# Moving the wait for the output from SyncE to GpSimd at the end of a decode kernel, without GpSimd's closing drain

## The chip, the cores and the metric

The kernel runs on one core of a Trainium2 chip. The time is device microseconds of one execution. "The span" is the time from the first to the last instruction of the program that the profile shows; the measured time is longer than the span.

Names: PE is TensorE, DVE VectorE, ACT ScalarE, POOL GpSimd, SP SyncE; SPq or POOLq is an engine's sequencer, which carries out branches, drains and semaphore instructions. L578 is line 578 of the kernel.

## The reference

One decode step of a transformer layer for four sequences, in bfloat16: layer norm, attention with 32 heads over a cache of 4096 positions, output projection, residual; then layer norm, a SwiGLU feed-forward block, residual.

```python
def reference(A_x, A_k_cache, A_v_cache, A_wq, A_wo, B_x, B_w_gate, B_w_up, B_w_down):
    x = A_x                                                     # (4, 1, 640)
    h = x + _A_ref(_layernorm(x), A_k_cache, A_v_cache, A_wq, A_wo)   # caches (4, 32, 4096, 192)
    h2 = h + _B_ref(_layernorm(h), B_w_gate, B_w_up, B_w_down)  # 640 -> 1536 -> 640
    return h2
```

## The kernel before

SP streams the K and V caches in loads of 6 MB, DVE and PE work on them in loops. None of that is touched. What matters is the end: the last cast, four small output DMAs (two issued by SP, two by ACT), and a recording layer that writes each engine's program into one block. SP is the engine that waits for the output.

```python
    def emit(self, block, final):
        # ... dependencies become semaphore values (cut)
        def run(eng):
            def body(e):
                # ... this engine's instructions with their waits (cut)
                if eng == "sp":
                    for d in final:
                        e.wait_ge(d.sem, d.value)
            return body
        block.vector(run("dve")); block.gpsimd(run("pool")); ...   # (cut)

    # ... end of build_kernel:
    a = op("dve", lambda e: e.tensor_copy(out=outsb[:, 0:DQ], in_=psH[:, 0:DQ]), [a])
    fin = [dma("sp" if n < 2 else "act", lambda e, n=n: e.dma_start(
        out[:, 0, n * DQ:(n + 1) * DQ], outsb[32 * n:32 * n + B, 0:DQ]), S_out, [a]) for n in range(4)]

    with nc.Block() as block:
        pr.emit(block, [fin[-1]])
```

The end of a block is a barrier, which the built program spells out. Each engine branches to the block's end (the profiles show a branch only where it carries a wait). DVE, ACT, PE and SP drain, and the drain's semaphore update is the engine's arrival. GpSimd drains, collects the four arrivals (one semaphore instruction) and releases the others (a second one). The others pass (one each). "Arrival", "collect", "release" and "pass" are used for these below. SP's wait for the output is attached to SP's branch.

## Time and profile before

| | before |
|---|---|
| measured time, median of the first three runs | 989.99 us (989.90 to 990.32) |
| measured time of the profiled run, its span | 989.84 us, 988.26 us |
| HBM traffic | 424.29 MB read, 429 GB/s |
| last cast ends, output landed, last pass | 985.89, 987.66, 988.26 us |

Lines of the profile page before: the span; busy time by engine; the main DMA queue with packets, MB and its share of sixteen engines' span; the chain of work that ended last, by engine.

```profile
span 988.3 us, 9469 instructions
...
PE 579.3 (59%) x4409; PEld 129.0 (13%) x2941; DVE 553.3 (56%) x454; ACT 117.1 (12%) x376; POOL 3.7 (0%) x18
...
q1 hardware_dynamic: 10528, 424.29, 99.5%
...
DMA 67%; PE 18%; DVE 12%; issue 1%; SPq 1%; DVEq 0%
```

DMA is busy from end to end, no engine is; the kernel is bound by its 424 MB. GpSimd does 3.7 us of work, all at the start.

The instructions of the closing line before. The columns are engine and operation, count, duration in ns (lowest, median, highest), and the start of the first and the last in us.

```profile
L578 POOLq EVENT_SEMAPHORE  x2: 17/17/17, 987.9 to 987.9; - x2
L578 POOLq DRAIN  x1: 611/611/611, 4.9 to 4.9; - x1
...
L578 ACTq DRAIN  x1: 239/239/239, 986.8 to 986.8; - x1
L578 SPq COMPARE_BRANCH  x1: 33/33/33, 987.7 to 987.7; - x1
L578 SPq DRAIN  x1: 7/7/7, 987.8 to 987.8; - x1
L578 ACTq EVENT_SEMAPHORE  x1: 17/17/17, 988.0 to 988.0; - x1
L578 PEldq EVENT_SEMAPHORE  x1: 51/51/51, 988.0 to 988.0; - x1
L578 DVEq EVENT_SEMAPHORE  x1: 21/21/21, 988.0 to 988.0; - x1
L578 SPq EVENT_SEMAPHORE  x1: 17/17/17, 988.2 to 988.2; - x1
```

Two lines of SP's waits before (who waited for whom, us in total, times, longest):

```profile
SPq L578 <- DMA out_dram<-gu: 1.1, 1, 1.1
SPq L578 <- SPq L578: 0.4, 1, 0.4
```

GpSimd's drain ran at 4.9 us. SP's branch comes when the output has landed, at 987.7. Everyone passes at 988.0 but SP, which passes at 988.2 and so ends the span; the second wait line is that lateness, seen from SP's drain.

The view rounds starts to 0.1 us. Where finer times stand below, they are the records of the trace, in us after the landing of the last output increment (987.661 before): branch of SP 0.017, its drain 0.158, collect 0.190, release 0.269, passes of ACT, PE, DVE 0.315 to 0.322, pass of SP 0.586, end of span 0.603. SP's branch is recorded only once its wait is over. This agrees with the Trainium skill, "Perfetto Trace Analysis", section "Sequencer-only Instruction (DRAIN, etc)": the profiler reports such an instruction from when its semaphores are satisfied.

### The profile page before, as it was taken

To read this page: it belongs to the slowest core of one execution; us is meant where nothing else is said; L and a number is where in the kernel's file an instruction comes from. 1 tells how busy PE (TensorE), PEld (TensorE's weight loads), DVE (VectorE), ACT (ScalarE), POOL (GpSimd) and SP (SyncE) were. 2 spreads that over 40 slices of the span, in tenths; PEclk is the share of its full clock that TensorE was granted. 3 is DMA by queue.
4 is the path that set the end of the run, shared out by engine and by line. 5 is a ranking of instruction groups with operands and counts; after the bars stand their busy time and mean duration, and the time that the engine had idled before them with its cause. 6 is when DMAs were issued, how large, how long until landed. Compare 5 with 4: busy or idle time off the path is not lost.

```text
span 988.3 us, 9469 instructions
## 1 busy us (share of the span) xinstructions
PE 579.3 (59%) x4409; PEld 129.0 (13%) x2941; DVE 553.3 (56%) x454; ACT 117.1 (12%) x376; POOL 3.7 (0%) x18
## 2 busy tenths in 40 slices
PE   1677555666555576556566655656665555765554
PEld 0011011110101111001111110111101011110023
DVE  2486555566645556655556665555666455566621
ACT  0311111110111110011111011111101111100120
POOL 1000000000000000000000000000000000000000
PEclk9898777887777888777788777788877778887775
DMA  9999999999999999999999999999999999999997
GB/s 401 428 440 426 434 436 426 440 434 430 436 426 440 434 432 436 426 438 434 432 436 426 438 434 432 436 426 438 434 432 436 426 438 434 432 436 426 438 433 327
DMA packets 10583, 424.39 MB, mean 429 GB/s; under 512 B 1232, under 2 KB 1232, under 8 KB 1744
## 3 DMA queue, kind: packets, MB, share of 16 engines
q1 hardware_dynamic: 10528, 424.29, 99.5%
q8 instruction: 5, 0.08, 0.0%
q10 hardware_dynamic: 48, 0.01, 0.0%
q14 instruction: 2, 0.02, 0.0%
HBM read 424.29 MB, written 0.01 MB: 429 GB/s over the span
## 4 chain that ended last, share of the span: by engine, by line
DMA 67%; PE 18%; DVE 12%; issue 1%; SPq 1%; DVEq 0%
DMA k<-in_A_k_cache_dram 63%; DVE prod L412 12%; PE pb L161 11%; PE pb L462 4%; DMA wd_sb<-in_B_w_down_dram 4%; PE pb L420 2%; SPq L365 0%; DVE sc L425 0%; PE pb L468 0%; DVEq L412 0%; SPq L391 0%; SPq L385 0%; PE pb L571 0%; SPq L330 0%; PE pb L434 0%
## 5 line engine op out<-in xcount | busy, mean ns | idle before, releaser
L412 DVE TENSOR_TENSOR prod<-k,qball 128x6144 f16<-128x6144 bf16 x128 | 426.3, 3351 | 220.9 <-DMA k<-in_A_k_cache_dram 220.9
L161 PE MATMUL pb<-prod,identH 128*128 128x512 f16 x1408 | 384.3, 429 | 0.0
L420 PE MATMUL pb<-prod,identH 128*128 128x512 f16 x128 | 58.1, 454 | 339.9 <-DVE prod L412 339.9
L425 DVE TENSOR_REDUCE sc<-pb 128x32 f32<-128x512 f32 x128 | 88.0, 688 | 107.2 <-PE pb L161 107.2
L477 ACT ACTIVATE otmp<-pb,minv 128x192 f32<-128x192 f32 x32 | 13.4, 420 | 650.8 <-PE pb L462 650.8
L420 PEld LDWEIGHTS pb<-prod,identH 128*128 128x128 f16 x128 | 13.2, 103 | 586.1 <-DVE prod L412 481.2
L462 PE MATMUL pb<-v,pbuf 128*8 128x384 bf16 x1984 | 86.0, 326 | 0.0
L453 ACT ACTIVATE pbuf<-sc,negM 32x128 bf16<-32x128 f32 x128 | 73.4, 574 | 4.9
L462 PEld LDWEIGHTS pb<-v,pbuf 128*8 128x8 bf16 x1984 | 45.4, 87 | 28.8
L481 DVE SCALAR_TENSOR_TENSOR orow<-pb,minv,otmp 128x192 f32<-128x192 f32 x32 | 13.4, 418 | 55.1 <-ACT otmp L477 55.1
L497 PEld LDWEIGHTS pb<-orow,here 128*128 128x128 f32 x256 | 33.5, 192 | 73.7 <-issue 71.1
L497 PE MATMUL pb<-orow,here 128*128 128x48 f32 x256 | 31.7, 267 | 1.1 <-DVE orow L481 1.1
L453 ACT ACTIVATION_READ_ACCUMULATOR pbuf<-sc,negM 32x1 f32 x128 | 31.7, 248 | 0.0
L447 ACT ACTIVATE negM<-pb 128x4 f32<-128x4 f32 x32 | 5.5, 173 | 161.0 <-PE pb L443 161.0
L468 PEld LDWEIGHTS pb<-lsb,headm 128*128 128x128 f32 x64 | 12.3, 194 | 74.8 <-issue 71.2
L443 PE MATMUL pb<-negMc,ones_row 1*128 1x4 f32 x64 | 12.2, 258 | 11.9 <-DVE negMc L438 11.9
L434 PE MATMUL pb<-identF,msb 128*1 128x128 f32 x64 | 12.1, 270 | 9.8 <-DVE msb L430 9.8
L438 DVE TENSOR_REDUCE negMc<-pb 1x4 f32<-1x128 f32 x32 | 8.9, 279 | 15.1 <-PE pb L434 15.1
L443 PEld LDWEIGHTS pb<-negMc,ones_row 1*128 1x128 f32 x64 | 9.4, 183 | 21.3 <-DVE negMc L438 21.3
L468 PE MATMUL pb<-lsb,headm 128*128 128x1 f32 x64 | 9.2, 213 | 2.7 <-ACT pbuf L453 2.7
L490 ACT ACTIVATE here<-place 128x131 f32 (+1 forms) x32 | 10.0, 312 | 0.9
L430 DVE TENSOR_REDUCE msb<-sc 128x1 f32<-128x128 f32 x32 | 9.1, 286 | 1.1
(68 smaller groups left out, 84.8 us busy)
## 6 DMA issues: line engine op xcount, KB each, us to landing
k<-in_A_k_cache_dram SPq DMA_DIRECT2D x32, 6144.0 KB, 39.5
v<-in_A_v_cache_dram SPq DMA_DIRECT2D x31, 6144.0 KB, 25.5
wq_sb<-in_A_wq_dram SPq DMA_DIRECT2D x1, 7680.0 KB, 21.5
k<-in_A_v_cache_dram SPq DMA_DIRECT2D x1, 6144.0 KB, 39.2
wo_sb<-in_A_wo_dram SPq DMA_DIRECT2D x1, 5760.0 KB, 25.0
wo_sb<-in_A_wo_dram SPq DMA_DIRECT2D x1, 1920.0 KB, 26.9
wg_sb<-in_B_w_gate_dram SPq DMA_DIRECT2D x1, 1920.0 KB, 31.2
wu_sb<-in_B_w_up_dram SPq DMA_DIRECT2D x1, 1152.0 KB, 33.5
```

Of the source, the lines that this page charges most:

```text
L161: return e.add_instruction(mybir.InstMatmult(name=e.bass.get_next_instruction_name(), engine=mybir.EngineType.PE, start_tensor_calc=start, ...
L412: op("dve", lambda e: e.tensor_tensor(out=prod[BUF[k]][:, :, :], in0=kslot[u % 2][:, k * QT:(k + 1) * QT, :], in1=qball[:, bass.ds(u + pr. ...
L420: op("pe", lambda e, j=j: (e.matmul if j == 0 else partial(held_matmul, e))(psR[k][:, 0:QT * R], lhsT=identH[:, :], rhs=prod[BUF[k]][:, :, ...
L425: op("dve", lambda e: e.tensor_reduce(sc[u % 2][:, k * QT:(k + 1) * QT], psR[k][:, 0:QT * R].rearrange("q (t r) -> q t r", r=R), AX.X, ALU ...
L434: op("pe", lambda e: e.matmul(psS[0:1, XT], lhsT=msb[:, 0:1], rhs=identF[:, :], start=True, stop=True), [g("rmax", u), g("negM", u - 1), p ...
L443: op("pe", lambda e: e.matmul(psS[:, XB], lhsT=ones_row[0:1, :], rhs=negMc[0:1, :], start=True, stop=True), [g("hmax", u), g("negM", u - 1 ...
L453: op("act", lambda e, h=h, r=r: e.activation(out=pbuf[r, :, h], in_=sc[u % 2][r, :], func=ACTF.Exp, bias=negM[r, h:h + 1], scale=alpha, ac ...
L462: op("pe", lambda e, t=t, n=n: e.matmul(psO[32 * n:32 * n + 8, 0:2 * DH], lhsT=pbuf[:, t:t + 2, :].rearrange("q t m -> q (t m)"), rhs=vsrc ...
L468: op("pe", lambda e: e.matmul(psS[:, XL], lhsT=headm[:, :, :].rearrange("q r m -> q (r m)"), rhs=lsb[:, :], start=True, stop=True), [g("ex ...
L477: op("act", lambda e: e.activation(out=otmp[:, :], in_=psO[:, 0:DH], func=ACTF.Copy, scale=minv[:, 0:1]), [g("pv", u), g("minv", u), g("st ...
L481: op("dve", lambda e: e.scalar_tensor_tensor(out=orow[:, :], in0=psO[:, DH:2 * DH], scalar=minv[:, 1:2], in1=otmp[:, :], op0=ALU.mult, op1 ...
L497: op("pe", lambda e, i=i: e.matmul(psT[:, bass.ds(JW * at_unit(u)[0], JW)], lhsT=here[:, NI - 1 - i:NI - 1 - i + 128], rhs=orow[:, JW * i: ...
```

## The change

The intent is to shorten the end: GpSimd, which leads the closing barrier and has nothing else to do, waits for the output itself, and its drain is left out.

```diff
-    def emit(self, block, final):
+    def emit(self, block, closer, final):
...
-                if eng == "sp":
+                if eng == closer:
                     for d in final:
                         e.wait_ge(d.sem, d.value)
...
-    with nc.Block() as block:
-        pr.emit(block, [fin[-1]])
+    with nc.Block(no_gpsimd_drain=True) as block:
+        pr.emit(block, "pool", fin[-1:])
```

In the built program the option does two things. GpSimd's drain goes; and the drains of the four other engines no longer carry the arrival, which becomes a separate semaphore instruction after each drain.

## The prediction

> **What bounds the kernel now.** DMA. The page gives 424.39 MB at a mean of 429 GB/s, and the main DMA queue takes 99.5% of sixteen engines' span. The chain that ended last is 63% K loads. The change touches none of that: up to the end of the block the five engines' programs are the same, instruction by instruction.
>
> **The end of the program before** (view of the closing line, exact times from the trace's records). The last product is cast by 985.89 us; the four output DMAs are issued from 985.92; the last of their semaphore increments lands at 987.66. SP, which waits for it, branches at 987.68 (33 ns) and drains at 987.82 (7 ns); that drain carries SP's arrival at the closing barrier. GpSimd collects the arrivals at 987.85 and releases at 987.93; ACT, PE and DVE pass at 987.98. SP passes only at 988.25, which ends the span. SP's waits show the same: 1.1 us for the output, 0.4 us between drain and pass. GpSimd's own drain, which the change deletes, ran at 4.93 us for 611 ns behind its last memset; GpSimd then idled for 982 us. So the deleted drain is worth nothing.
>
> **What the change does.** (1) The wait for the output and the branch after it move from SP to GpSimd. (2) GpSimd's drain goes. (3) The other four engines' drains no longer carry the arrival; each gets one more semaphore instruction (17 to 51 ns), while the output is still in flight: SP is free at 986.59, ACT's drain ends at 987.02, so all should have arrived by 987.1 to 987.5, before 987.66. (4) After the landing, SP's drain and the hop from SP to GpSimd leave the chain; landing, GpSimd's branch, collect, release and everybody's pass remain.
>
> **Cost.** Before: landing to end 0.60 us. After, if GpSimd's branch costs what SP's did (0.14 us to the next instruction) and its two semaphore instructions stay 0.08 us apart: collect 987.82, release 987.90, passes 987.95 to 988.03, which is 0.25 us less. Only 0.03 us of that is the removed hop; 0.22 us is SP's late pass (0.29 us after the release where the others took 0.02 to 0.03). I take that for something SP pays just after its branch. If GpSimd pays it too, between collect and release, the gain is about zero. Estimate, weighing both: 0.15 us gained.
>
> The time of the profiled run (989.84 us) is 1.6 us more than its span. The Trainium skill, "Runtime: NRT & Kernel Launch", section "The ~15µs preamble/postamble breakdown", puts a barrier (about 1.5 us) and semaphore resets (about 1.5 us) after a kernel; this trace shows semaphores written from 988.70 to 989.96, so the tail has that form. It should start earlier by what the span gains.
>
> **Predicted time:** 989.8 us, 8 in 10 within 989.3 to 990.3 (three runs before spread over 0.42 us, more than the effect). Faster by over 2%: 0.003; within 2%: 0.994; slower by over 2%: 0.003.
>
> **What the profile should show.** Busy times, GB/s and chain as before; GpSimd without its drain near 4.9 us, with a branch about 1.76 us after the output's issue; SP's branch and drain near 986.7; all passes within 0.1 us of the release; landing to end 0.35 to 0.6 us.
>
> **What would make it wrong.** GpSimd waking from its wait much slower than SP did, or taking over 1 us from the branch to the next instruction; the closing work after the span depending on GpSimd more than on SP; or a chance shift of the K stream by over 0.5 us.

## The result, and the profile after

| | before | after |
|---|---|---|
| median of six runs each | 990.06 us (989.75 to 990.32) | 990.43 us (990.01 to 990.53) |
| ratio, 95% interval | | 1.0003 (0.9990 to 1.0016) |
| profiled run: measured time, span | 989.84, 988.26 | 990.01, 988.19 |
| measured time minus span | 1.58 us | 1.82 us |
| landing of the output to end of span | 0.603 us | 0.371 us |
| landing of the output to end of measured time | 2.179 us | 2.192 us |

The ratio is the mean time of one kernel's runs over that of the other's of the same rounds, so it is not quite the ratio of the medians quoted here. The last row is the measured time of the profiled run less the time of the landing in its trace.

The same lines of the page after:

```profile
span 988.2 us, 9471 instructions
...
PE 580.5 (59%) x4408; PEld 128.9 (13%) x2941; DVE 553.4 (56%) x454; ACT 117.1 (12%) x376; POOL 3.7 (0%) x18
...
q1 hardware_dynamic: 10528, 424.29, 99.5%
...
DMA 68%; PE 17%; DVE 12%; issue 1%; SPq 1%; DVEq 0%
```

The closing line after, columns as before:

```profile
L578 PEldq EVENT_SEMAPHORE  x2: 51/51/51, 985.8 to 988.1; - x2
L578 DVEq EVENT_SEMAPHORE  x2: 21/21/21, 986.1 to 988.1; - x2
L578 SPq EVENT_SEMAPHORE  x2: 17/17/17, 987.1 to 988.1; - x2
L578 ACTq EVENT_SEMAPHORE  x2: 17/17/17, 987.2 to 988.1; - x2
L578 POOLq EVENT_SEMAPHORE  x2: 17/17/17, 988.0 to 988.1; - x2
...
L578 SPq DRAIN  x1: 221/221/221, 986.8 to 986.8; - x1
...
L578 POOLq COMPARE_BRANCH  x1: 33/33/33, 987.8 to 987.8; - x1
```

And the line of SP's waits that answers to the two of before:

```profile
SPq L578 <- PEq L578: 1.1, 1, 1.1
```

The block's end looks as it was meant to. Nothing of it is left at 4.9 us, SP arrives at 987.1 (the first of its two semaphore instructions), GpSimd branches when the output has landed (987.8), and all passes start at 988.1. The span's tail after the landing is 0.232 us shorter. And yet the measured time did not move: measured time minus span grew by 0.245 us. The gain was given back behind the last instruction that the profile shows. This is no accident of the profiled run. Measured time minus span (the span is given to 0.1 us) is 1.51 to 1.63 us in every later run of the kernel before, and 1.75 to 1.83 us in all eleven runs of the changed one.

Two questions are left. What does the closing work behind the span follow, if not the last pass? And is the 0.37 us between the two medians real?

**Theory 1 (a hold that moved).** An engine that branches late, after its long wait, is held up once, until about 0.57 us after the branch. SP paid this before its pass. GpSimd pays it now, after its last instruction and so outside the span. The closing work waits for the held engine.

**Theory 2 (slack).** The closing work follows GpSimd's release by a fixed time, and that release did not move. SP's late pass was slack.

The records have a clue. The Trainium skill, "Runtime: NRT & Kernel Launch", section "Semaphores 0–2 are reserved", says that semaphore 2 is the runtime's sync barrier. In the trace semaphore 2 takes two groups of nine increments around and after the end of the program (before: from 0.612 to 1.150 us after the landing, and, behind writes to nearly all other semaphores, from 1.940 to 2.297). Below, "first" to "fifth increment" are those of the first group. Before, the first five come at 0.612, 0.646, 0.858, 0.901 and 0.925 us after the landing; after, at 0.607, 0.641, 0.851, 0.894 and 0.918. They hardly moved. GpSimd's release did not move either: 0.269 before, 0.267 after.

The last increment of the second group also checks the measure used below. It comes 0.115 to 0.127 us after what this document takes as the end of the measured time, in all 14 profiled runs. So differences between runs in "landing to end" are differences of the closing work, and not of something that the measured time might hold before the span.

### The profile page after: what moved, and what is told of

It is laid out like the page before. It is cut to its first block, busy times and chain, and to the rows that moved or that the text cites. A ratio compares the mean times of both kernels' runs of the same rounds, so it can differ in the third digit from the quotient of the medians.

```text
span 988.2 us, 9471 instructions
## 1 busy us (share of the span) xinstructions
PE 580.5 (59%) x4408; PEld 128.9 (13%) x2941; DVE 553.4 (56%) x454; ACT 117.1 (12%) x376; POOL 3.7 (0%) x18
## 4 chain that ended last, share of the span: by engine, by line
DMA 68%; PE 17%; DVE 12%; issue 1%; SPq 1%; DVEq 0%
DMA k<-in_A_k_cache_dram 64%; DVE prod L412 12%; PE pb L161 11%; PE pb L462 4%; DMA wd_sb<-in_B_w_down_dram 4%; PE pb L420 2%; SPq L365 0%; DVE sc L425 0%; PE pb L468 0%; DVEq L412 0%; SPq L385 0%; SPq L391 0%; PE pb L571 0%; SPq L330 0%; PE pb L434 0%
```

## The experiments

Edits are shown against the changed kernel. "Landing to end" stands for the landing of the output to the end of the measured time of the profiled run. Three batches ran on three chips (e1 to e4, e5 to e8, e9 to e12), each compared with the kernel before of the same rounds. e5, e6, e9, e10 and e12 had one round, two executions each (medians 990.27, 990.15, 990.03, 990.21 and 989.38 us); only their traces are used.

### e1_null_before and e2_after_again: both kernels again

No edit.

> The kernel before, unchanged, as a test of the comparison itself. If the 0.37 us by which the changed kernel's median was higher is chance of the K and V stream, this copy can come out 0.2 to 0.4 us off the kernel before too; if runs of one program repeat to 0.1 us, its ratio is 1.0000 within 0.0001 and the 0.37 us needs a cause. In the profile: landing of the output to the end of the measured time 2.18 us, as before.

> The changed kernel, unchanged, in more rounds. Chance: within 0.2 us of the kernel before. A real loss: again 0.3 to 0.4 us slower, with an interval that leaves out 1. All theories: landing to last pass 0.37 us, landing to the end of the measured time 2.19 us, so measured time minus span 1.8 us against 1.55 us for the copy of before.

Measured: the copy of before 990.25 us (989.74 to 990.72, five runs), ratio to the kernel before 1.0002 (0.9988 to 1.0016). The changed kernel 990.30 us (989.98 to 990.45, five runs), ratio 1.0002 (0.9988 to 1.0015). Landing to end 2.169 and 2.166 us; end of span after the landing 0.602 and 0.371 us, as the first time.

The same program compared with itself differs as much as the change does. Over all rounds the kernel before ran 33 times, from 989.72 to 990.92 us, mean 990.21; the changed kernel's eleven runs have a mean of 990.32. The traces give the two ends of the program the same cost within 0.03 us (2.179 and 2.169 us against 2.192 and 2.166). The medians of the kernel before in the four batches lie 0.35 us apart (990.06 to 990.41), so 0.37 us between medians of six runs is within what one program shows. A difference of 0.1 us before the landing can't be excluded by these runs.

### e3_sp_nodrain: the option alone, SP waits as before

```diff
-        pr.emit(block, "pool", fin[-1:])
+        pr.emit(block, "sp", fin[-1:])
```

> SP waits as before; only GpSimd's drain goes, and the arrivals become separate semaphore instructions. Theory 1 (an engine that branches late is held up once, until about 0.57 us after its branch, and the closing work after the span waits for it): SP's arrival at the barrier is held to about 0.59 us after the landing, release about 0.68, last pass about 0.73, landing to end of measured time about 2.3 us. Theory 2 (the closing work starts 0.31 us after GpSimd's release, SP's late pass was slack): nothing holds SP's arrival (about 0.21), release about 0.3, landing to end of measured time about 2.2 us, SP passing late again or not without effect.

Measured: 990.39 us (ratio 1.0003, 0.9989 to 1.0017). The closing line of this run (GpSimd and SP):

```profile
L578 SPq EVENT_SEMAPHORE  x2: 17/17/17, 988.4 to 988.5; - x2
L578 POOLq EVENT_SEMAPHORE  x2: 17/17/17, 988.4 to 988.5; - x2
...
L578 SPq COMPARE_BRANCH  x1: 33/33/33, 987.8 to 987.8; - x1
L578 SPq DRAIN  x1: 7/7/7, 988.0 to 988.0; - x1
```

SP drains at 988.0 and its next instruction, the arrival, starts only at 988.4, though in the built program it waits for nothing but a semaphore that is still zero. In finer times: drain 0.156, arrival 0.563, release 0.688 us after the landing. So SP is held for 0.4 us after its late drain; that half of theory 1 is right. But landing to end was 2.586 us, where theory 1 said 2.3. The closing work followed the later release, as in theory 2: its first increment came 0.37 us after the release, against 0.34 us in the traces of before and after (and 0.37 us in e1, the copy of before).

This also shows that the option alone makes the end worse by 0.41 us. It moves SP's arrival off the drain, to behind SP's hold.

### e4_pool_drain: GpSimd waits, its drain stays

```diff
-    with nc.Block(no_gpsimd_drain=True) as block:
+    with nc.Block() as block:
```

> GpSimd waits, but its drain stays and now stands between its branch and its collect. Theory 1: the second instruction after the late branch is held up, so collect at about 0.59 us after the landing, release 0.67, last pass 0.72, landing to end of measured time about 2.3 us. Theory 2: drain 0.19, collect 0.22 to 0.27, release 0.3 to 0.35, landing to end of measured time 2.2 to 2.25 us.

Measured: 990.27 us (ratio 1.0002, 0.9989 to 1.0016). Branch 0.024, drain 0.173 (41 ns), collect 0.258, release 0.336, landing to end 2.230 us. GpSimd is not held after its late branch. The drain, now behind the wait, costs 0.07 us of release and 0.05 us of end.

### e5_pool_marks and e6_sp_marks: extra instructions after the barrier

Waits that are already true were put behind the barrier, on one engine at a time. They show in the records when the engine gets to its next instructions, and they delay what follows on that engine.

```diff
         pr.emit(block, "pool", fin[-1:])
+    for _ in range(8):
+        nc.gpsimd.wait_ge(S_out, fin[-1].value)     # e6: nc.sync instead
```

> The changed kernel with eight more waits on GpSimd after the barrier; each is true already, so they only show in the records when GpSimd gets to its next instructions. Theory 1 (GpSimd, which now branches late, is held up as SP was, only after the end of the span): the marks are even, about 0.08 us apart, but for one gap of about 0.3 us near 0.55 to 0.6 us after the landing. Theory 2 (the closing work follows GpSimd's release by 0.34 us whoever waited): all eight even, about 0.08 us apart, no gap. If the closing work waits for GpSimd, landing to end of measured time grows by their sum, about 0.65 us, from 2.18 to about 2.8; if it waits for another engine, it stays at 2.2.

> The changed kernel with the same eight waits on SP after the barrier, some 0.04 to 0.08 us each, 0.3 to 0.6 us in all. If SP's late pass before was slack of about 0.28 us or more (theory 2), landing to end of measured time grows by the sum less 0.28 us, so by 0 to 0.3 us, to at most 2.5; if the closing work follows SP directly, it grows by the whole sum.

The eight waits were merged into four instructions with two waits each. On GpSimd:

```profile
L581 POOLq EVENT_SEMAPHORE  x4: 43/43/43, 988.0 to 988.3; - x4
```

Measured on GpSimd: the four start 0.363, 0.454, 0.541 and 0.628 us after the landing, with no gap. Nothing is left of theory 1 for GpSimd. GpSimd's last instruction ended 0.387 us later than in the changed kernel, and landing to end grew to 2.516 us, by 0.32 us (0.35 us over e2, the copy). The first two increments of semaphore 2 stayed at 0.607 and 0.641; the third moved from 0.851 to 1.203. GpSimd's release had not moved (0.267), so theory 2 needs a correction: the closing work follows GpSimd's last instruction, not its release.

On SP:

```profile
L581 SPq EVENT_SEMAPHORE  x4: 28/28/28, 988.1 to 988.3; - x4
```

Measured on SP: the four end at 0.642 us, later than SP's late pass in the kernel before. Landing to end stayed at 2.198 us, and all five increments stayed where they were. So SP's pass at 0.603 us in the kernel before was slack.

### e9_sp_marks24: more on SP than the slack holds

As e6, with 24 waits (twelve instructions).

> Three times as many waits on SP after the barrier as in the run before that had eight: these were merged into four instructions, some 0.07 us apart, and SP was done 0.64 us after the landing without any cost. Twelve instructions should end at about 1.2 us after the landing, past the 0.85 us at which GpSimd joins the closing barrier. If the barrier takes the later of GpSimd's last instruction plus 0.57 us and SP's plus about 0.07 us, the third increment of its semaphore comes at about 1.25 us instead of 0.85, and landing to end of measured time is about 2.6 us. If SP plays no part in it, 2.18.

```profile
L581 SPq EVENT_SEMAPHORE  x12: 27/28/28, 988.0 to 988.7; - x12
```

Measured: the twelve end at 1.124 us. The third and fourth increments stayed at 0.851 and 0.894; it was the fifth that moved, from 0.918 to 1.245, 0.12 us after SP's last instruction. Landing to end was 2.424 us, less than the 2.6 that was expected, since SP joins the barrier later in the row than was assumed.

### e10_act_closes: ACT waits

```diff
-        pr.emit(block, "pool", fin[-1:])
+        pr.emit(block, "act", fin[-1:])
```

> As the run in which SP waits and branches without GpSimd's drain (there SP's arrival was held to 0.56 us after the landing), but with ACT as the engine that waits. If the hold after a late branch is SP's alone: ACT's arrival at about 0.2 to 0.25, release about 0.3, landing to end of measured time about 2.2 us. If ACT is held up the same way: arrival about 0.55, release about 0.68, end 2.55 to 2.6 us. Either way GpSimd's release plus 1.9 us should give the end.

```profile
L578 ACTq EVENT_SEMAPHORE  x2: 17/17/17, 988.0 to 988.2; - x2
...
L578 ACTq COMPARE_BRANCH  x1: 38/38/38, 987.8 to 987.8; - x1
L578 ACTq DRAIN  x1: 8/8/8, 988.0 to 988.0; - x1
```

Measured: branch 0.021, drain 0.181, arrival 0.228, release 0.358, landing to end 2.284 us. ACT is not held after a late branch; so far the hold of 0.4 us was seen on SP alone. The release plus 1.9 us gives 2.26.

### e7_sp_after and e8_pool_after: the barrier first, then the wait

If the closing work follows GpSimd's release, the release should come early. Here no engine waits for the output inside the block. All go through the barrier while the output is in flight, and one engine waits behind it, so the program still ends only after the output has landed.

```diff
-        pr.emit(block, "pool", fin[-1:])
+        pr.emit(block, None, fin[-1:])
+    nc.sync.wait_ge(S_out, fin[-1].value)           # e8: nc.gpsimd instead
```

> All five engines go through the block's barrier while the output is still in flight; SP alone then waits for the output after the barrier, with nothing after that wait. Theory 2 with slack on SP: the release comes about 0.5 us before the landing and the closing work starts as soon as SP is through, so landing to end of measured time about 1.6 us, 0.55 us less than 2.18, and at most 1.9. A theory in which the closing work starts a fixed 0.6 us after the output's landing, whatever the program does: still 2.18. In the measured time 0.3 to 0.6 us out of 990 is at the edge of what five rounds show.

> The same with GpSimd as the one that waits after the barrier. If the closing work needs 0.34 us after GpSimd's last instruction, landing to end of measured time is about 2.18 - 0.27 + 0.02 = 1.93 us, so 0.25 to 0.35 us more than with SP. If the 0.34 us belongs to the other engines, it is about 1.6 us, as with SP.

The closing line of e7 (SP and GpSimd), SP's wait behind the barrier (L580), and a line of SP's waits:

```profile
L578 SPq EVENT_SEMAPHORE  x2: 17/17/17, 987.2 to 987.7; - x2
...
L578 POOLq EVENT_SEMAPHORE  x2: 17/17/17, 987.4 to 987.5; - x2
```

```profile
L580 SPq EVENT_SEMAPHORE  x1: 17/17/17, 988.0 to 988.0; - x1
```

```profile
SPq L578 <- SPq L578: 0.5, 1, 0.5
```

Measured, with SP waiting: release 0.479 us before the landing, SP through 0.034 us after it, landing to end 1.419 us, which is 0.76 us less than before and more than the 0.55 us expected. The measured median was 989.39 us against 990.30 (ratio 0.9991, 0.9977 to 1.0004). With GpSimd waiting: landing to end 1.888 us, median 989.60 us (ratio 0.9995, 0.9982 to 1.0009). The guess for SP was too high because it took SP for the engine that the closing work would wait for. The third increment came at 0.105 us, which is again 0.567 us after GpSimd's last instruction: the two paths now end nearly together.

The last of these lines shows something else. In e7, e8, e11 and e12 no engine's branch waits for the output, and still SP passes the barrier only 0.165 to 0.177 us after the release, where ACT, DVE and PE pass after 0.045 to 0.054 us. SP's own instruction before it, its arrival, had ended 0.434 to 0.445 us earlier. So SP stands still for 0.4 us there too, and a late branch is not needed for it.

### e11_sp_after_again and e12_sp_after_drain

e11 is e7 again. e12 adds a drain and eight true waits on SP behind the wait:

```diff
     nc.sync.wait_ge(S_out, fin[-1].value)
+    nc.sync.drain()
+    for _ in range(8):
+        nc.sync.wait_ge(S_out, fin[-1].value)
```

> The version in which SP waits after the barrier, again, on whatever chip comes. Landing to end of measured time again 1.42 us, measured time minus span 1.35 to 1.45 us; measured median about 0.75 us less than the kernel before of the same rounds (ratio about 0.9992), with chance of the K and V stream of 0.3 us on either.

> The same, with a drain on SP that carries the wait for the output, and then eight true waits (four instructions), to see whether it is the drain or the branch after which SP stands still. If the drain holds it: a gap of about 0.4 us between the drain and the first of the four. If it was the late branch: the four follow at once, 0.07 us apart, and SP is through about 0.35 us after the landing, so landing to end of measured time is 1.42 + 0.3 = about 1.7 us.

Measured, e11: landing to end 1.424 us, median 989.34 us against 990.41 (ratio 0.9990, 0.9976 to 1.0003). The ten runs of this version in e7 and e11 lie between 989.06 and 989.73 us, the 33 of the kernel before between 989.72 and 990.92. The intervals of the ratios still touch 1, so the gain is settled by the tail in the traces (0.76 us both times), not by the ratio.

Measured, e12: SP's drain at 0.017 took 7 ns, and the four marks followed at 0.086, 0.160, 0.227 and 0.286 us, without a gap. A drain that ends a long wait does not hold SP by itself. But SP had already stood still once in this run, before its pass, so a hold that comes only once, at the block's end, is not excluded. The fifth increment came at 0.426 us, 0.11 us after SP's last instruction, and landing to end was 1.645 us.

### What the traces say together

Worked out from the records of each trace, in us after the landing:

```
run                  GpSimd's last  third       SP's last  fifth       landing
                     instr. ends    increment   instr.     increment   to end
before                  0.286        0.858       0.603      0.925       2.179
e1  before again        0.285        0.857       0.602      0.925       2.169
after                   0.284        0.851       0.326      0.918       2.192
e2  after again         0.284        0.851       0.325      0.918       2.166
e3  SP waits, option    0.705        1.272       0.747      1.339       2.586
e4  drain kept          0.353        0.914       0.395      1.044       2.230
e5  marks on GpSimd     0.671        1.203       0.325      1.270       2.516
e6  marks on SP         0.284        0.851       0.642      0.918       2.198
e9  more marks on SP    0.283        0.851       1.124      1.245       2.424
e10 ACT waits           0.375        0.943       0.418      1.011       2.284
e7  SP after barrier   -0.462        0.105       0.034      0.172       1.419
e11 e7 again           -0.462        0.106       0.034      0.173       1.424
e8  GpSimd after        0.041        0.579      -0.299      0.645       1.888
e12 e11, marks on SP   -0.470        0.098       0.314      0.426       1.645
```

The third increment follows GpSimd's last instruction by 0.53 to 0.57 us in every run. Where SP is not late, the end of the measured time follows that increment by 1.31 to 1.35 us. The fifth increment comes 0.07 us after the third, except in e9 and e12, where SP is late, and in e4. In e4 it came 0.130 us after the third, though SP's last instruction had ended 0.65 us before it (why, is not known), and neither the sixth increment nor the end was later for it. So in these runs SP mattered only where its last instruction plus 0.12 us was later than about the third increment plus 0.13 us, as in e9 and e12.

## Why the prediction was right or wrong

- **Bound by DMA, stream untouched: right.** Busy times, traffic and the shares of the chain are the same to a percent.
- **The deleted drain is worth nothing: right, for the kernel before.** It ran at 4.93 us. Kept behind GpSimd's wait it would cost 0.05 us (e4). What was missed is that the option also puts the other engines' arrivals behind their drains, which costs 0.41 us where SP still waits (e3). The two edits are no sum: the option alone loses 0.41 us, the move alone 0.05 us, both together nothing.
- **The block's end: right.** The prediction computed 0.25 us less from landing to last pass if GpSimd pays no hold. Measured 0.232 us, with the passes within 0.053 us of the release.
- **The hop from SP to GpSimd as a gain of 0.03 us: wrong, and not noticed.** GpSimd woke at 0.024 us where SP woke at 0.017, and took 0.162 us from branch to next instruction where SP took 0.141. That ate the hop, and the release stayed where it was (0.269 and 0.267).
- **The step that failed** is, as the prediction put it, that the closing work after the span "should start earlier by what the span gains". It follows GpSimd's last instruction by 0.57 us, and SP's late pass, which ended the span, had slack in that time. GpSimd's last instruction ended at 0.286 us before and at 0.284 us after. The gain in the span was therefore worth 0.00 us instead of the 0.15 us estimated. Marks on GpSimd alone moved the end (e5), marks on SP alone did not until they were longer than the slack (e6, e9). The prediction's list of what could go wrong had named this ("the closing work after the span depending on GpSimd more than on SP"), without weighing it.
- **The measured time lay 0.13 us above the range.** The range was centred too low and too narrow. 0.15 us of it was the gain that did not come. About 0.2 us was the base: the median of the three runs at hand was 989.99 us, the mean of 33 is 990.21. The rest, 0.26 us, is put down to chance of the stream, which no run shows by itself. The profiled runs of e7 and e11, one program on two chips, end their last cast at 986.20 and 985.88 us; a spread of 0.42 us in three runs was too small a sample to set the range by.

What stays open: why SP stands still for 0.4 us at the block's end, after its drain (before, e3) or after its arrival (e7, e8, e11, e12). A late branch is not needed for it, and ACT and GpSimd do not show it after one (e10, e4). A fetch of instructions would be one candidate, but the traces of before and e3 have no packet of an instruction queue during the hold. This does not touch the main result, which needs only that SP's pass came late, and not why. That the third increment of semaphore 2 is GpSimd's and the fifth SP's is inferred from their moving with marks on these engines and on no other. Marks on ACT, PE and DVE were not tried.

## What to carry to other kernels

The profile's last instruction need not be what ends the measured time: compare measured time minus span before and after, and if the one shrinks by what the other grows, nothing was won. On this program the closing work followed GpSimd, so what pays is to let GpSimd leave early. Take the block's barrier while the output is still in flight and let SP alone wait for the output behind it, which took 0.76 us off the tail. When an effect is smaller than the run-to-run spread, measure it inside the trace, from one fixed event (here the landing of the output) to the end.

## What the Trainium skill lacked or had wrong

- "Runtime: NRT & Kernel Launch", section "The ~15µs preamble/postamble breakdown", gives the closing barrier about 1.5 us and the semaphore resets after it, as the prediction quotes, about 1.5 us; here the barrier's nine increments were through 0.86 us after GpSimd's last instruction (after), and the writes to the other semaphores took 0.67 us from first to last (before). The page's 44 ns for a hop, given for the barrier before a kernel, agrees: the second group of nine takes 0.357 us (before), 45 ns for each of eight hops. What it lacks is that GpSimd's increment comes 0.53 to 0.57 us after its last instruction and SP's, where SP is late, 0.11 to 0.12 us after, so that it matters which engine ends last (1.42 us from landing to end with SP last, 1.89 with GpSimd).
- The same page, same section, calls the gap between the profile's total time and the execution time kernel-invariant (about 6.2 us). There the profile's total is the longer of the two, while here the measured time is longer than the span, so it is another quantity and no run here tests it. What the page lacks is that measured time minus span varies with how the program ends: 1.30 to 1.85 us in the profiled runs.
- "VectorE: DVE Perf Modes", section "The DRAIN you can't avoid", says that boilerplate drains, those put around a kernel, are about 12 ns on all engines. What it lacks is the program's own drains at the end of a block. They took 7 ns on an engine that had long been idle (SP, before), but 221 ns on SP just after a DMA issue (after), about 480 ns on PE, and 611 ns on GpSimd behind a memset.
- No page that I read has SP's standstill of 0.4 us at the end of a block (0.400 us in e3, 0.435 us in e7), nor that ACT and GpSimd don't show it where they wait for the output (e10, e4).
